# Holding expert 1's weight loads on GpSimd behind the last pair's row copies and two late transposes, in a sparse attention kernel with a routed mixture of experts

## The chip, the cores and the metric

The kernel runs on one core of one Trainium2 chip. The metric is the device time of one execution in microseconds (us), lower is better. Before the change three runs took 671.94, 671.15 and 670.29 us, median 671.15.

The engines are named as the profile names them: PE is TensorE (PEld its weight loads), DVE VectorE, ACT ScalarE, POOL GpSimd, SP SyncE. GpSimd and SyncE issue the DMAs that matter here: GpSimd those that load from DRAM with a cast to 16 bits, SyncE the small copies within the on-chip memory (SBUF) and the transposes by DMA. A name such as L464 is a line of the kernel before; the lines after the changed place stand 11 lower in the changed file.

## What is computed

Attention over 4 batches x 8 heads x 768 positions of width 64, in which each query sees its neighbours at a distance under 16 and one summary for each of 24 blocks of 32 positions (the maximum of the keys, the mean of the values). Then a mixture of 8 experts over all 3072 rows, in which every expert runs on every row and the weights of the routing come from eight rounds of Sinkhorn normalization:

```python
mask_l = np.abs(pos[:, None] - pos[None, :]) < window          # window 16
scores_s = scale * einsum('bhsd,bhnd->bhsn', q, k_sum) + log(block)
a = softmax(concat([where(mask_l, scores_l, -1e9), scores_s]))
x = matmul(a, concat([v, v_sum]))                              # to (3072, 512)
P = exp(x @ w_gate - max)
for _ in range(8):
    P /= P.sum(1, keepdims=True) + 1e-09
    P /= P.sum(0, keepdims=True) + 1e-09
    P *= N / E
for e in range(E):                                             # 8 experts, 512 -> 1024 -> 512
    out += P[:, e:e + 1] * (np.maximum(x @ w1[e], 0) @ w2[e])
```

## The kernel before

**Stages.** The heads are taken in 16 pairs (pair i: two heads of batch i // 4). Pairs 0 to 3 are worked in halves, pairs 4 to 15 whole. Expert 0 needs no routing weight until later, so its two matmuls fill TensorE between the attention's steps (`hps` L221 the hidden layer, `yps` L231 the projection). Up to 128 us or so the profile shows this mixture. Then come the eight Sinkhorn rounds with the end of expert 0 and the beginning of expert 1 woven in, and from 169 us experts 1 to 7, whose products are made with seven half-size products in place of eight (L972 and L978).

**A planner writes the order.** In the first two stages each step is a unit with an engine, an estimated cost, the units it depends on and a priority (`add`). The planner (`Plan.order`) takes the estimates and lists the units in one order; the order of each engine's instructions follows from it and is fixed when the kernel is built. On the chip the engines then wait for each other with semaphores that follow from the tiles that are read and written. `load` adds three units: the issue on POOL, which follows the issue before it, a DMA's duration, and the landing `U[key]`, on which others can depend. Loads are thus issued by GpSimd in the order in which they are added.

**A whole pair** (pairs 4 to 15). Keys and queries are transposed to `kT`, `qT` (from pair 12 on by DMA on SyncE, L354). `scores` makes the neighbour scores (`sg` L383), `score_exp` and `masks` make `em`. `near_values` copies rows of the values from the neighbouring 128-row chunks into `Ve`: four DMAs of 10.2 KB on SyncE, two on L414 and two on L416, for the two heads. `Ve` has two buffers, which alternate. `edges` makes the matching products `Ee` on VectorE (L443, L447). `values` sums it up in `av`: L458 with `em`, then L464 with `Ee` and `Ve`, so that L464 needs all four copies. `normalize` (L546, L547) writes `xs`, which has two buffers for whole pairs: pair i writes where pair i - 2 wrote, once that one has been transposed to `xT`. For pairs 10 to 14 this transpose is a DMA on SyncE (`x_dma`, L358); pair 15's is made on TensorE (`tx` L554) and copied by ScalarE. SyncE's queue has, at the end: `xT` of pair 11, four copies of pair 14, `xT` of pair 12, four copies of pair 15, `xT` of pair 13, `xT` of pair 14.

After the last pair, `logits` (`lp` L568) reads all of the last batch's `xT`; ScalarE makes `P_sb` of it (L572), with which the Sinkhorn rounds begin: row sums and reciprocals on VectorE (L1169, L1170), a product on GpSimd (L1173), column sums on VectorE (L1177), their total on TensorE (`sink` L1182), its reciprocal on VectorE (L1185) and a product on GpSimd (L1190).

**Expert 1's weights.** They are the last loads on GpSimd: `load_w1(1, i)` for i = 0 to 3 (two DMAs of 128 KB each, L197) and `load_w2(1)` (one of 1024 KB, L208). Ahead of them stands `hold`: four one-element copies on GpSimd that read `qT` of pairs 12 to 15 (L885), and so wait until those transposes have landed. On VectorE the sums for the half-size products follow the last normalization: `w1_sum` of the four groups (reading `w`, writing `ws`) and `x_sum` (L919 `xTs`), in this order: groups 0 and 1, the first `x_sum`, group 2 with the second `x_sum` in it, group 3; then the row sums of Sinkhorn. The tiles `xTs`, `ws` and `hf` lie where the attention's tiles lay, `held` among them. TensorE's first products of expert 1 are `pa` (reading `w`) and `pb` (reading `ws` and `xTs`).

Of the kernel before, what the change touches and what calls it, by code (L numbers as in the profile page):

```python
# [10 lines left out]
BF16 = mybir.dt.bfloat16  # L11
# [23 lines left out]
class Plan:  # L35
# [13 lines left out]
    def add(self, eng, cost, fn, deps=(), prio=0.0, opens=(), uses=(), lag=0.0, shape=None):  # L49
        u = Unit(eng, cost, fn, [d for d in deps if d is not None], prio, list(opens), lag, shape)  # L50
        for b in list(opens) + list(uses):
            b.users.append(u)
        if uses and eng != "PE":
            u.prio -= 100.0
        self.waiting.append(u)
        return u
# [80 lines left out]
def kernel(  # L137
# [10 lines left out]
    nc = tc.nc  # L148

    B, H, S, D = q.shape  # L150
# [7 lines left out]
    NP = (B * H) // 2  # L158
    PB = H // 2
# [5 lines left out]
    VD = D + 1  # L165
# [15 lines left out]
    xT = persist.tile([128, KD, N], FP16)  # L181
# [11 lines left out]
    def load_w1(e, i):  # L193
        t = w1s[e, i] = wpool.tile([128, KD, 2, 128], FP16, tag="w1", name="w1", bufs=5)
        for h in range(2):
            f = h * (F // 2) + 128 * i
            nc.gpsimd.dma_start(out=t[:, :, h, :],  # L197
                                in_=moe_w1[e].rearrange("(dk p) f -> p dk f", p=128)[:, :, f:f + 128])
# [7 lines left out]
    def load_w2(e):  # L206
        w2s[e] = wpool.tile([128, KF, DM], FP16, tag="w2", name="w2")
        nc.gpsimd.dma_start(out=w2s[e][:], in_=moe_w2[e].rearrange("(fk p) d -> p fk d", p=128))  # L208
# [28 lines left out]
    NE = 2  # L237
# [8 lines left out]
    attn = early.enter_context(tc.tile_pool(name="attn", bufs=1))  # L246
    aps = early.enter_context(tc.tile_pool(name="aps", bufs=1, space=PSUM))
    if True:

        ident = attn.tile([128, 128], BF16, name="ident")  # L250
        held = attn.tile([1, 1], BF16, name="held")
        band = attn.tile([128, LIVE], BF16, name="band")
        m_blk = attn.tile([128, 4 * (G - 1) + 128], BF16, name="m_blk")
        qT = [attn.tile([128, W + S + W], BF16, name=f"qT{i}") for i in range(NB)]
# [10 lines left out]
        V_e = [attn.tile([128, G, 2 * VD], BF16, name=f"Ve{i}") for i in range(NE)]  # L265

        plan = Plan({"m": 3, "s": NS, "a": NA})
        add = plan.add
# [319 lines left out]
        def keep_busy(n):  # L588

            t = bank("m", "idle")  # L590
            for _ in range(n):
                nc.tensor.matmul(t[:], lhsT=zeros[:], rhs=zeros[:, None, :].to_broadcast([128, 4, 128]), start=True, stop=True)
# [74 lines left out]
        U = {}  # L667
        last = [None, None]

        def load(key, fn, issue, us, deps=(), late=False):  # L670
            last[0] = add("POOL", issue, fn, [last[0], *deps])
            last[1] = add("DMA", us, None, [add("RING", 0, None, [last[0]], lag=0.8), last[1]])
            U[key] = add("LAND", 0, None, [last[1]], lag=1.0 if late else 0.4)
# [209 lines left out]
        def hold():  # L883
            for r in range(12 % NB, NB):
                nc.gpsimd.tensor_copy(out=held[0:1, 0:1], in_=qT[r][0:1, W:W + 1])  # L885

        last[0] = add("POOL", 0.3, hold, [last[0]] + [U["kT", i, 1] for i in range(12, NP)])
        for i in range(4):
            load(("w1n", i), lambda i=i: load_w1(1, i), 0.85, 1.3)
        load("w2n", lambda: load_w2(1), 0.85, 5.0)  # L890
        plan.idle = (0.22, lambda: keep_busy(1), U["rl", 0, 0])
        attention = {u for u in plan.waiting if u.fn is not None} - set(zero)
# [11 lines left out]
    if True:  # L904
# [32 lines left out]
        def weight1(what, e, i):  # L937
            if what in ("S1", "S2", "S4"):
                return ws1[e, i][:, "S1 S2 S4".split().index(what), :, :]
            k = KH if what in ("A12", "A22") else 0  # L940
            return w1s[e, i][:, k:k + KH, int(what in ("A21", "S3", "A22")), :]

        def w1_sum(e, i, n):
            if n == 0:
                ws1[e, i] = fast.tile([128, 3, KH, 128], FP16, tag="ws1", name="ws1", bufs=5)
            m = {w: weight1(w, e, i) for w in "A11 A12 A21 A22 S1 S2 S3 S4".split()}
            f, o, a, b = ((plus, "S1", "A21", "A22"), (sub, "S2", "S1", "A11"), (sub, "S3", "A11", "A21"),
                          (sub, "S4", "A12", "S2"))[n]
            f(m[o], m[a], m[b])
# [209 lines left out]
        def bridge():  # L1159
# [39 lines left out]
            X, Wt = {}, {}  # L1199
# [5 lines left out]
                                  [X.get((j, n - 1))] + hs0, 990.0 + 100 * j + n)  # L1205
            for i in range(4):
                for n in range(4):
                    Wt[i, n] = add("DVE", 0.3, lambda i=i, n=n: w1_sum(1, i, n), [Wt.get((i, n - 1))],
                                   980.0 + 5 * i + n)
            step2 = None  # L1210
            for n in range(4):
# [2 lines left out]
            for i in range(4):  # L1214
                f = made[1, 0, i] = group(1, 0, i)
                a, b, g = Buffer("ab"), Buffer("ab"), Buffer("g")
                k5, k2 = Buffer("c5"), Buffer("c2")
                d = {}

                def op(name, eng, us, deps, opens=(), uses=()):  # L1220
                    d[name] = add(eng, us, f[name], [d[x] if isinstance(x, str) else x for x in deps],
                                  1000.0 + PRI[i], opens=opens, uses=uses)

                op("p1", "PE", 0.44, [], [a])
                op("seed", "ACT", 0.58, ["p1"], [g], [a])
                op("p5", "PE", 0.44, ["p1", Wt[i, 0], X[0, 0]], [b])
                op("c5", "ACT", 0.58, ["p5"], [k5], [b])
                op("p2", "PE", 0.44, ["seed"], (), [a])
                op("r11", "ACT", 0.58, ["p2"], (), [a])
                op("p6", "PE", 0.44, ["seed", Wt[i, 1], X[0, 1]], (), [g])  # L1230
                op("c2", "ACT", 0.58, ["p6"], [k2], [g])
                op("p3", "PE", 0.44, ["c5", Wt[i, 3]], (), [b])
                op("c12", "DVE", 0.68, ["p3", "c2"], (), [b, k2])
                op("p7", "PE", 0.44, ["c2", X[0, 2]], (), [g])
                op("c22", "DVE", 0.68, ["p7", "c5"], (), [g, k5])
                op("p4", "PE", 0.44, ["c22", X[0, 3]], (), [g])
                op("r21", "ACT", 0.58, ["p4"], (), [g])
                op("r12", "DVE", 0.3, ["c12"])
                op("r22", "DVE", 0.3, ["c22"])
                op("s1", "DVE", 0.42, ["r12", "r22"])  # L1240
                op("s3", "DVE", 0.42, ["s1", "r11"])
                op("s2", "DVE", 0.42, ["s1"])
                op("s4", "DVE", 0.42, ["s2", "r21"])

        groups = [(e, j, i) for e, j in steps for i in range(4)]
        LAG = 4
        made, PRI, PW = {}, (5.05, 5.5, 6.05, 6.5), 1007.0
        bridge()
        for u in course:
            if u.fn is not None:  # L1250
# [5 lines left out]
        for n in range(LAG, len(groups)):  # L1256
# [3 lines left out]
            e, j, i = groups[n]  # L1260
# [48 lines left out]
        last = [pair(*groups[len(groups) - LAG + n], spare=bool(n % 2), c1_at=c1s[n], tail=True) for n in range(LAG)]  # L1309
# [49 lines left out]
```

## Time and profile before

| What | us |
|---|---|
| median of three runs | 671.15 |
| the profiled execution, its own time | 674.88 |
| the span in it, first to last instruction | 673.2 |
| TensorE busy in the span | 661.4 |
| VectorE, ScalarE, GpSimd busy | 581.9, 399.7, 129.5 |
| first `w1` issue of expert 1 on GpSimd | 94.54 |
| pair 15's four row copies issued | 102.44 to 104.56 |
| `av` L464 of pair 15 starts | 116.04 |
| first `w1_sum` on VectorE | 117.88 |
| first `pa` of expert 1 on TensorE | 128.10 |

Times inside the span are counted from its start. Timelines have the start, the duration, the engine, the line, what is done (out<-in) and how often; in brackets the idle time ahead and what ended it. The page cuts the span into 40 slices of 16.8 us:

```profile
PE   8999998999999999999999999999999999999996
DVE  8889897677799988998799988998899879998885
POOL 8699440122101010201010010101020101100001
DMA  9999989000513050311422051305031132201224
```

The DMA engines are nearly full for the first six slices, some 100 us, and mostly empty behind. VectorE is busy at 60 to 90% throughout, TensorE nearly all the time.

### The profile page before, as it was taken

The numbers are of one execution on the slowest core, as the hardware profiler recorded it, in microseconds if no ns is written. First come the engines' busy times: TensorE is split into PE (matmuls) and PEld (weight loads), VectorE is DVE, ScalarE is ACT, GpSimd is POOL, SyncE is SP. The second block draws the span as 40 slices with busy tenths as digits, with TensorE's granted clock in tenths as the row PEclk, the third lists the DMA queues.
The fourth block names the chain that finished last, engine by engine and source line by source line (L and its number), as shares of the span: only waits on it lengthen the run. The fifth ranks groups of instructions, "written<-read, shape, count | busy, mean of one in ns | idle before, by whom it ended". The sixth has DMA issues, their size and how long they took to land.

```text
span 673.2 us, 13510 instructions
## 1 busy us (share of the span) xinstructions
PE 661.4 (98%) x5077; PEld 436.4 (65%) x5077; DVE 581.9 (86%) x1475; ACT 399.7 (59%) x782; POOL 129.5 (19%) x175
## 2 busy tenths in 40 slices
PE   8999998999999999999999999999999999999996
PEld 4766655555666666666666666666666666666665
DVE  8889897677799988998799988998899879998885
ACT  6776674565777765555655565555555565556551
POOL 8699440122101010201010010101020101100001
PEclk9999999999999999999999999999999999999999
DMA  9999989000513050311422051305031132201224
GB/s 159 184 150 147 143 97 142 1 1 1 78 11 39 1 79 1 36 14 20 61 23 25 1 79 12 37 1 79 1 36 14 27 52 23 26 1 56 86 80 157
DMA packets 124033, 36.75 MB, mean 55 GB/s; under 512 B 110144, under 2 KB 121152, under 8 KB 123968
## 3 DMA queue, kind: packets, MB, share of 16 engines
q0 software_dynamic: 104128, 25.93, 41.3%
q1 hardware_dynamic: 18880, 9.22, 6.7%
q8 instruction: 40, 0.66, 0.4%
q10 hardware_dynamic: 960, 0.74, 0.3%
q14 instruction: 25, 0.20, 0.1%
HBM read 52.45 MB, written 6.29 MB: 87 GB/s over the span
## 4 chain that ended last, share of the span: by engine, by line
PE 88%; DVE 6%; DMA 5%; issue 0%; ACT 0%; DVEq 0%; ACTq 0%
PE xy L978 37%; PE pg L972 16%; PE pa L972 11%; PE pb L972 11%; PE yps L231 5%; PE hps L221 4%; DMA Ve<-vx 3%; DMA kT<-kst 1%; DVE xs L547 1%; DMA vx<-in_v_dram 1%; PE sg L383 1%; PE tkq L349 1%; PE tx L554 0%; DVE km L377 0%; PE vs L393 0%
## 5 line engine op out<-in xcount | busy, mean ns | idle before, releaser
L978 PEld LDWEIGHTS <-hf 128*128 128x128 f16 x2352 | 230.1, 98 | 95.8 <-issue 0.8
L978 PE MATMUL xy<-w,hf 128*128 128x256 f16 x1312 | 183.4, 273 | 0.0
L978 PE MATMUL xy<-ws,hf 128*128 128x256 f16 x984 | 147.6, 273 | 0.1
L212 ACT ACTIVATE hf<-pg 128x512 f16<-128x512 f32 x84 | 50.1, 597 | 151.3 <-PE pg L972 151.2
L1114 DVE SCALAR_TENSOR_TENSOR out_acc<-xy,P_sb,out_acc 128x512 f32<-128x512 f32 x164 | 115.0, 742 | 2.1 <-PE xy L978 2.1
L919 DVE TENSOR_TENSOR hf<-hf 128x512 f16<-128x512 f16 x252 | 100.2, 425 | 8.9 <-DVE hf L922 0.5
L972 PE MATMUL pa<-xT,w 128*128 128x512 f16 x336 | 99.9, 379 | 0.0
L972 PEld LDWEIGHTS <-w 128*128 128x128 f16 x672 | 65.8, 98 | 43.5
L922 DVE TENSOR_TENSOR hf<-pb,c 128x512 f16<-128x512 f32 x84 | 58.1, 691 | 36.8 <-PE pb L972 34.5
L197 POOL DMA_DIRECT2D w<-in_moe_w_dram x56 | 41.7, 756 | 220.1 <-PE pg L972 191.7
L972 PEld LDWEIGHTS <-ws 128*128 128x128 f16 x504 | 49.3, 98 | 25.1
L1006 ACT COPY c<-pg 128x512 f32<-128x512 f32 x84 | 49.2, 586 | 22.4 <-PE pg L972 22.4
L922 DVE TENSOR_TENSOR hf<-pg,c 128x512 f16<-128x512 f32 x84 | 57.1, 679 | 0.7 <-PE pg L972 0.7
L212 ACT ACTIVATE hf<-pa 128x512 f16<-128x512 f32 x84 | 50.6, 603 | 0.9 <-PE pa L972 0.9
L991 ACT COPY pg<-pa 128x512 f32<-128x512 f32 x84 | 47.9, 570 | 4.9
L972 PE MATMUL pg<-xT,w 128*128 128x512 f16 x168 | 50.0, 379 | 0.0
L972 PE MATMUL pb<-xTs,ws 128*128 128x512 f16 x168 | 50.0, 379 | 0.0
L972 PE MATMUL pg<-xTs,ws 128*128 128x512 f16 x168 | 50.0, 379 | 0.0
L972 PE MATMUL pb<-xT,ws 128*128 128x512 f16 x168 | 50.0, 379 | 0.0
L972 PE MATMUL pg<-xTs,w 128*128 128x512 f16 x168 | 50.0, 379 | 0.0
L999 ACT COPY c<-pb 128x512 f32<-128x512 f32 x84 | 49.8, 593 | 0.0
L221 PE MATMUL hps<-xT,w 128*128 128x384 f16 x256 | 48.9, 326 | 0.0
(150 smaller groups left out, 829.9 us busy)
## 6 DMA issues: line engine op xcount, KB each, us to landing
w<-in_moe_w_dram POOLq DMA_DIRECT2D x8, 1024.0 KB, 9.5
w<-in_moe_w_dram POOLq DMA_DIRECT2D x56, 128.0 KB, 3.4
out_dram<-out_acc SPq DMA_DIRECT2D x20, 256.0 KB, 2.0
vx<-in_v_dram POOLq DMA_DIRECT2D x16, 192.0 KB, 5.8
qst<-in_q_dram POOLq DMA_DIRECT2D x31, 96.0 KB, 5.0
kst<-in_k_dram POOLq DMA_DIRECT2D x24, 96.0 KB, 5.4
w<-in_moe_w_dram POOLq DMA_DIRECT2D x2, 512.0 KB, 9.3
Ve<-vx SPq DMA_DIRECT2D x48, 10.2 KB, 4.6
```

The lines of the kernel that those rows point to most:

```text
L197: nc.gpsimd.dma_start(out=t[:, :, h, :], in_=moe_w1[e].rearrange("(dk p) f -> p dk f", p=128)[:, :, f:f + 128])
L212: nc.scalar.activation(out=out, in_=in_, func=AF.Relu, bias=0.0, scale=1.0)
L221: nc.tensor.matmul(hp[:, 0:n], lhsT=w1s[e][:, dk, 128 * f:128 * (f + 1)], rhs=xT[:, dk, t0:t0 + n], start=(dk == 0), stop=(dk == KD - 1))
L231: nc.tensor.matmul(yp[:], lhsT=h[:, f, c * 128:(c + 1) * 128], rhs=w2s[e][:, f, :], start=(f == 0), stop=(f == KF - 1))
L919: nc.vector.tensor_tensor(out=out, in0=in0, in1=in1, op=ALU.subtract)
L922: nc.vector.tensor_tensor(out=out, in0=in0, in1=in1, op=ALU.add)
L972: nc.tensor.matmul(bank[:], lhsT=w[:, dk, :], rhs=x[:, dk, :], start=start and dk == 0, stop=dk == KH - 1, skip_group_check=True)
L978: nc.tensor.matmul(bank, lhsT=a(f)[:, 128 * c:128 * (c + 1)], rhs=w[:, f, :], start=start and f == 0, stop=f == FH - 1, skip_group_check=True)
L991: nc.scalar.copy(out=B["g"][:], in_=B["a"][:])
L999: nc.scalar.copy(out=B["c5"][:], in_=B["b"][:])
L1006: nc.scalar.copy(out=B["c2"][:], in_=B["g"][:])
L1114: nc.vector.scalar_tensor_tensor(out=acc, in0=src, scalar=P_sb[:, t, e:e + 1], in1=acc, op0=ALU.mult, op1=ALU.add)
```

## The change

`held` grows from one element to 128 partitions x 1. Two new functions read more into it on GpSimd. `hold_near` reads, for each of the two heads, one column of the 32 rows of `Ve` that pair 15's copies write, and then calls `hold_x(12)`, which reads one element of pair 12's `xT`. It stands ahead of the four `w1` loads. `hold_x(14)` reads one element of pair 14's `xT` and stands between the `w1` loads and the `w2` load. Each copy waits for the DMAs that write what it reads, and what stands behind it on GpSimd waits with it. For the planner the new units depend on the landings of those DMAs, and `w1_sum` and `p1` of expert 1 now depend on the landing of their `w1` load.

```diff
-        held = attn.tile([1, 1], BF16, name="held")
+        held = attn.tile([128, 1], BF16, name="held")
...
+        def hold_near():
+            for j in range(2):
+                p = 64 + 32 * j
+                nc.gpsimd.tensor_copy(out=held[p:p + 32, 0:1], in_=V_e[(NP - 1) % NE][p:p + 32, 1, VD * j:VD * j + 1])
+            hold_x(12)
+
+        def hold_x(i):
+            nc.gpsimd.tensor_copy(out=held[0:1, 0:1], in_=xT[0:1, i % PB, i // PB * S:i // PB * S + 1])
+
         last[0] = add("POOL", 0.3, hold, [last[0]] + [U["kT", i, 1] for i in range(12, NP)])
+        last[0] = add("POOL", 0.4, hold_near, [last[0], U["near", NP - 1], U["x", 12]])
         for i in range(4):
             load(("w1n", i), lambda i=i: load_w1(1, i), 0.85, 1.3)
+        last[0] = add("POOL", 0.2, lambda: hold_x(NP - 2), [last[0], U["x", NP - 2]])
         load("w2n", lambda: load_w2(1), 0.85, 5.0)
...
-                    Wt[i, n] = add("DVE", 0.3, lambda i=i, n=n: w1_sum(1, i, n), [Wt.get((i, n - 1))],
+                    Wt[i, n] = add("DVE", 0.3, lambda i=i, n=n: w1_sum(1, i, n), [Wt.get((i, n - 1)), U["w1n", i]],
...
-                op("p1", "PE", 0.44, [], [a])
+                op("p1", "PE", 0.44, [U["w1n", i]], [a])
```

## The prediction

> **What bounds the kernel now.** I read the page first, then the waits of TensorE, the chain of waits, the timeline around the longest wait and the granted clock by microsecond. The page's busy line and its chain line:
>
> ```profile
> PE 661.4 (98%) x5077; PEld 436.4 (65%) x5077; DVE 581.9 (86%) x1475; ACT 399.7 (59%) x782; POOL 129.5 (19%) x175
> PE 88%; DVE 6%; DMA 5%; issue 0%; ACT 0%; DVEq 0%; ACTq 0%
> ```
>
> TensorE is busy for 661.4 of 673.2 us, so a change can gain only where it idles or runs slowly. The waits of TensorE (who waited for whom: total us, times, longest) name one wait that matters:
>
> ```profile
> PE av L464 <- DMA Ve<-vx: 2.9, 1, 2.9
> PE idle L592 <- DVE vx L600: 1.1, 1, 1.1
> PE tx L554 <- DVE xs L547: 0.3, 1, 0.3
> ```
>
> `av` (L464) of pair 15 waits 2.9 us for that pair's row copies into `Ve` (L414 and L416). In the chain of waits (start, us, what) the last pairs' copies are the two longest pieces of this stretch:
>
> ```profile
> 98.11 6.43 DMA Ve<-vx
> ...
> 104.56 11.35 DMA Ve<-vx
> 115.91 0.14 issue
> 116.04 0.40 PE av L464 x3
> ```
>
> Such a copy need not take 11 us. The DMA issues between 85.5 and 88.2 us, while GpSimd's queue was empty, and between 102.2 and 105 us, while it carried expert 1's weights (KB each, median us to landing):
>
> ```profile
> Ve<-vx SPq DMA_DIRECT2D x4, 10.2 KB, 1.9
> ...
> Ve<-vx SPq DMA_DIRECT2D x4, 10.2 KB, 11.8
> ```
>
> The timeline shows when those weights are issued (GpSimd) and what else waits: a normalization on VectorE, 2.34 us for the `xT` transpose of pair 12, which holds the `xs` buffer that pair 14 needs:
>
> ```profile
> 94.08 0.25 POOL L885 COPY held<-qT 1x1 bf16<-1x1 bf16 x1 [6.17 <-DMA qT<-qst]
> 94.54 5.94 POOL L197 DMA_DIRECT2D w<-in_moe_w_dram  x8 [0.21 <-issue]
> 100.40 0.96 POOL L208 DMA_DIRECT2D w<-in_moe_w_dram  x1
> ...
> 112.58 0.56 DVE L547 TENSOR_TENSOR xs<-av,rc 128x384 f16<-128x384 f32 x1 [2.34 <-DMA xT<-xs]
> 113.86 1.21 SPq L358 DMA_TRANSPOSE xT<-xs  x1
> ```
>
> Last the busy time by microsecond: window, its length, PE, PEld, DVE, ACT and POOL busy, then the granted clock.
>
> ```profile
> 115.00:116.00 1.00, 0.00 (x0) 0.00 (x0) 0.00 (x0) 0.00 (x0) 0.00 (x0) 1.00 0.99 193
> 116.00:117.00 1.00, 0.96 (x14) 0.79 (x15) 0.49 (x2) 0.00 (x0) 0.00 (x0) 1.00 0.04 6
> 117.00:118.00 1.00, 1.00 (x5) 0.38 (x3) 0.96 (x4) 0.00 (x0) 0.00 (x0) 0.54 0.00 0
> 118.00:119.00 1.00, 1.00 (x4) 0.34 (x3) 0.96 (x5) 0.59 (x1) 0.00 (x0) 0.50 0.00 0
> 119.00:120.00 1.00, 1.00 (x6) 0.56 (x5) 0.96 (x5) 0.00 (x0) 0.00 (x0) 0.50 0.00 0
> 120.00:121.00 1.00, 1.00 (x8) 0.58 (x6) 1.00 (x3) 0.52 (x1) 0.00 (x0) 0.75 0.00 0
> ```
>
> The wait has a second price: about one microsecond after it TensorE falls to half clock until 120.5 us, and counts as busy meanwhile. Lost are 0.46 + 0.50 + 0.50 + 0.25 = 1.71 us.
>
> **The change, part by part.** The built programs hold the same instructions in the same order on TensorE, VectorE, ScalarE and SyncE; GpSimd alone has four copies more. The new planner dependencies (`w1n`) thus move nothing. Of the waits one changes its meaning: the first `x_sum` on VectorE, which overwrites memory that `held` lies in, waited for the fourth `held` copy and now waits for the eighth.
>
> *Removed: the traffic of expert 1's weights between 96 and 115 us.* Pair 15's copies are issued at 102.44 to 104.4 us as before, since the first waits for TensorE's `av` of pair 13. Quiet copies take 1.9 us; copies queued right behind a transpose took 3.8 (median of those issued between 92.4 and 96.2 us). Pair 12's transpose is issued just ahead, at 100.76, so I take 3.8: landed by 108.2 (bound from below 106.3). TensorE wants them at 113.08 (the last `av` L458 starts at 112.91), so 4.9 us are spare. The next thing it needs there is pair 15's edge products, which stand behind the normalization of pair 14. Pair 12's transpose, quiet, takes 2.7 to 2.8 us and lands near 103.6, so VectorE's 2.34 us go as well and the edges end at 114.70 - 2.34 = 112.4, before 113.08. So the whole 2.93 us go, and with no gap before it I let the half clock go too: 1.71 us. Sum 4.64 us.
>
> At this place a rule speaks against the second term. The Trainium skill ("TensorE: Matmul & The Clock Gate", Part 1) has the clock fall back to half after at least one idle window of about 3.4 us, in windows that run free of the kernel. The gap here is 2.93 us and the clock was 0.50 behind it, so the trace doesn't agree with the length. By the rule alone the sum would be 2.93 us.
>
> *Added: four copies on GpSimd.* The `held` rows last 0.18 to 0.25 us; four are 0.9 us. They hide in GpSimd's idle 24.76 us before the first Sinkhorn product (L1173, 126.12 us).
>
> *Moved: eight `w1` issues.* GpSimd now waits for pair 15's copies and pair 12's transpose, so 106.3 to 108.2, then issues for 5.94 us: until 112.7 to 114.6 with the copies. Behind the waiting copies stand these loads, then the `w2` load, then Sinkhorn's products. Who needs the weights: VectorE's `w1_sum`, first at 117.88 before, now 2.9 us earlier, at 115.0; the fourth group about 119 to 120.5. Landing took 7.1 us in the median with the row copies and transposes beside it, 7.7 at most; 3.4 was the fastest. The first group lands by 109.8 + 7.1 = 116.9 at worst, the last by 114.6 + 7.7 = 122.3 at worst, near 117 if the traffic moves at the quiet pace. VectorE had 2.49 us free before the Sinkhorn row sums (125.28), and TensorE's `sink` product came 1.9 us after the column sums it needs (127.84 to 129.78). Half a microsecond to two is covered by these 4.4; I take 0.
>
> *Moved into the loads' traffic: the transpose of pair 14.* It is issued 2.34 us earlier, at 111.5, now amid the `w1` loads. Quiet it takes 2.7 us (114.2). Pair 11's, issued 2.2 us after the first `w1` load and beside `w1` traffic alone, took 6.7: 118.2. Pair 12's, with `w2` behind too, took 11.7. Of these the 6.7 is the nearest, since `w2` is now held behind this very transpose. TensorE first reads it in the gate's logits (`lp` L568, 124.26), now at 124.26 - 4.64 = 119.6: 1.4 us spare. VectorE's first `x_sum` (119.75, now 116.8 at the earliest) waits for the last `held` copy, 118.4, so 1.6 us; it comes out of the 2.49 above. Price 0; without cover 0 to 3.6, see the rivals.
>
> *Moved: `w2`.* Issued at 118.4 at the latest, with its own 14.5 us landed by 134. Its first reader on VectorE stood at 154.39, now 149.8. Price 0.
>
> Together: 674.88 (span 673.2 and 1.7 around it) - 4.64 = 670.2 for the profiled execution. The median of the runs, 671.15, lies 3.73 below the profiled time; taking the same 4.64 off it gives **666.5 us**.
>
> **The rivals.**
>
> *The half clock is not in the timed runs.* The three runs spread over 1.65 us, about one such loss. For it: the window is 3.4 us long (117.09 to 120.50) and its phase against the gap may differ. Against: the one trace has it. Gain 2.93: 668.2 us.
>
> *The 3.73 us by which the profiled execution is longer lie in this very stall.* For it: copies of 10 KB behind a full queue are what a disturbed execution delays first. Against: a profile also costs outside, and the queue is as full without one. Gain 4.64 - 3.73 = 0.9: 670.2 us.
>
> *The stall moves to pair 14's transpose.* If it takes pair 12's 11.7 us, it lands at 123.2, and the logits wait 3.6 us. With a half clock behind it that is 5.3 against 4.64 won: 671.8; without, 670.1. Against it: `w2`, which made the queue full to 115 us, is held.
>
> *Slower: the same wait, longer.* `w1`'s loads take the queue from the transpose as `w2` did, and it lands only after 14.5 us (`w2`'s own time), at 126.0. The logits wait 6.4 us, the half clock costs 1.7, and on VectorE `x_sum` and what stands behind it up to the row sums (some 3.5 us) end about 129.7 rather than 120.6. The column sums then end at 132.3, and `sink`, due at 129.78 - 4.64 + 8.1 = 133.2, is just covered: 8.1 - 4.64 = 3.5 slower, 674.6 us. It turns into a loss when the transpose lands later than 122.6 with the half clock, 124.3 without, 11 to 13 us after its issue. Against it: the eight loads moved for 12.8 us from first issue to last landing with everything beside them, and would end by 120 here.
>
> *The hold does not hold* can be left out: the two `Ve` reads cover what all four copies write, and the loads stand behind them on one engine.
>
> **How the numbers follow.** A measurement of this kernel can tell 0.3% from no change, 2.0 us, so faster means under 669.1. Full gain 0.52 (666.5), no half clock 0.22 (668.2), small stall in timed runs 0.10 (670.2), stall moved 0.11 (671), slower 0.05 (674.6). Faster 0.52 + 0.22 = 0.74; same 0.10 + 0.11 = 0.21; slower 0.05. The lower end takes the fastest run before, 670.29 - 4.64, and the two small waits at 93.42 and 104.82 us (0.26 and 0.20) as gone too: 665.2. The upper end takes in the small stall and the milder moved one: 670.4. Left out are the worse half of the moved stall and the slower case, about 0.11.
>
> **What would show it.** Right: `av` L464 of pair 15 starts within 0.3 us of the `av` before it; pair 15's copies land 2 to 4 us after their issue; no 0.50 in the granted clock between 113 and 125 us; `w1` issued from about 107; pair 14's transpose landed by 119; Sinkhorn 4.6 us earlier. Wrong: a wait of `lp` L568 for `xT`, of `sink` for the column sums, or `Ve` still landing after 113; the sum is also wrong if the gap goes and the time falls by 3 us only.

## The result: 0.27% faster, less than half of what was forecast

Twelve runs of each kernel: 671.58 us before (670.29 to 674.23), 669.95 us after (669.43 to 670.59). The ratio is 0.9973, 95% interval 0.9964 to 0.9982, so the change saves 1.2 to 2.4 us. The forecast was a saving of 4.64 us and 666.5 us. The measured time lies inside the forecast range of 665.2 to 670.4 us, near its upper end.

The page of the changed kernel, its busy line, the granted clock in 40 slices and the chain by engine:

```profile
PE 659.0 (99%) x5077; PEld 435.7 (65%) x5077; DVE 582.2 (87%) x1475; ACT 399.7 (60%) x782; POOL 131.8 (20%) x179
...
PEclk9999999999999999999999999999999999999999
...
PE 89%; DVE 7%; DMA 1%; ACT 1%; issue 1%; ACTq 0%; DVEq 0%
```

The span is 667.9 us. In the chain the share of DMA fell from 5% to 1%. TensorE's waits (who waited for whom: total us, times, longest) no longer have a line of `av` L464; the list begins (the first two stand in the span's first 5 us, the third at 64 us):

```profile
PE idle L592 <- DVE vx L600: 1.1, 1, 1.1
PE tkq L346 <- ACT kst L217: 0.4, 1, 0.4
PE tx L554 <- DVE xs L547: 0.3, 1, 0.3
```

The timeline of the changed kernel shows the holds on GpSimd and what they let through; in brackets, the idle time ahead and what ended it:

```profile
104.63 0.39 POOL L890 COPY held<-Ve 32x1 bf16<-32x1 bf16 x1 [11.22 <-DMA Ve<-vx]
...
105.94 1.41 POOL L890 COPY held<-Ve 32x1 bf16<-32x1 bf16 x1 [0.92 <-DMA Ve<-vx]
107.41 0.18 POOL L894 CAST held<-xT 1x1 bf16<-1x1 f16 x1
107.54 5.94 POOL L197 DMA_DIRECT2D w<-in_moe_w_dram  x8
...
112.31 0.35 PE L458 MATMUL av<-vx,em 128*128 128x65 bf16 x6
...
112.49 0.34 PE L464 MATMUL av<-Ve,Ee 128*128 128x130 bf16 x3
...
117.69 0.18 POOL L894 CAST held<-xT 1x1 bf16<-1x1 f16 x1 [4.21 <-DMA xT<-xs]
117.91 0.69 DVE L930 TENSOR_TENSOR xTs<-xT 128x1024 f16<-128x1024 f16 x1 [1.70 <-POOL held L894]
118.16 0.90 POOL L208 DMA_DIRECT2D w<-in_moe_w_dram  x1 [0.28 <-issue]
```

GpSimd stands still for 11.22 us, reads pair 15's rows at 104.63 and 105.94, and issues `w1` only from 107.54. In the list of DMA issues between 101.5 and 104.2 us the row copies now take 1.9 us, where they took 11.8:

```profile
Ve<-vx SPq DMA_DIRECT2D x4, 10.2 KB, 1.9
```

So `av` L464 follows the `av` before it without a wait, 112.49 after 112.31. Behind it, by microsecond (window, its length, busy time of PE, PEld, DVE, ACT and POOL, the granted clock), the clock stays at 1.00:

```profile
115.00:116.00 1.00, 1.00 (x10) 0.52 (x8) 0.96 (x6) 0.71 (x1) 0.00 (x0) 1.00 2.26 138
116.00:117.00 1.00, 1.00 (x6) 0.43 (x5) 0.21 (x2) 0.67 (x2) 0.00 (x0) 1.00 2.07 161
117.00:118.00 1.00, 1.00 (x6) 0.49 (x5) 0.09 (x1) 0.12 (x1) 0.18 (x1) 1.00 1.06 114
```

What the prediction named as signs of being right is there: no wait, no half clock, copies that land even sooner than in the 2 to 4 us expected, `w1` issued from 107.54, pair 14's transpose landed by 119, and Sinkhorn's first `sink` product even 5.3 us earlier. Between the two profiles the span fell by 673.2 - 667.9 = 5.3 us, more than was forecast. But the profiled execution of the kernel before, 674.88 us, is longer than all twelve of its runs here, while that of the changed kernel, 669.62 us, is one of its ordinary ones. What the experiments had to settle is how large the stall is in an ordinary execution of the kernel before.

### The profile page after: what moved, and what is told of

Its sections match the earlier page's. It is cut to its first block, busy times and chain, and to the rows that moved or that the text cites. A ratio compares the mean times of both kernels' runs of the same rounds, so it can differ in the third digit from the quotient of the medians.

```text
span 667.9 us, 13518 instructions
## 1 busy us (share of the span) xinstructions
PE 659.0 (99%) x5077; PEld 435.7 (65%) x5077; DVE 582.2 (87%) x1475; ACT 399.7 (60%) x782; POOL 131.8 (20%) x179
## 4 chain that ended last, share of the span: by engine, by line
PE 89%; DVE 7%; DMA 1%; ACT 1%; issue 1%; ACTq 0%; DVEq 0%
PE xy L989 37%; PE pg L983 16%; PE pa L983 11%; PE pb L983 11%; PE yps L231 5%; PE hps L221 5%; DVE xs L547 1%; DMA kT<-kst 1%; PE sg L383 1%; PE tkq L349 1%; DVE em L435 1%; DVE km L377 1%; DVE h L214 0%; DVE kh L375 0%; PE tx L554 0%
```

## The experiments

Two theories stood against each other. In the first, the first profile of the kernel before caught an unusually long stall, and in most executions the stall is short: the change removes all of it, but it is worth less. In the second, the stall of that profile is the usual one, and the changed kernel gives most of the gain back elsewhere (in the added waits, or in the loads that now come late).

**The kernel before, four more times.** No edit.

> The kernel before, unchanged, with the span and the mean granted clock of each timed run. Theory A (the profiled execution was a long one, in most runs pair 15's row copies land earlier): this profile shows a wait of L464 of 0.5 to 2 us and no half clock behind it, the spans scatter by 2 us or more, and the mean clock is 0.998 to 1.000 in most runs, 0.995 to 0.996 only in the longest. Theory B (the stall of 2.9 us and the half clock of 1.7 us are in every run, and the changed kernel gives 3 us back somewhere): a wait near 2.9 us again, a clock of 0.995 to 0.997 in nearly every run. Time as before, 671.6.

> The kernel before, unchanged, one more profile. With before (wait of L464 2.93 us, half clock behind it) and before_again (0.59 us, no half clock) it is a third sample of the wait. Theory A (the wait varies from execution to execution, mostly 0.5 to 2 us): a wait in that range, no half clock, pair 15's copies landed between 113 and 115. Theory B (2.9 us in most): 2.5 us or more.

> The kernel before, unchanged, for one more profile. If a short wait is the usual thing and the long one of the first profile rare: L464 of pair 15 waits 0.5 to 0.8 us, no half clock between 113 and 125 us, profiled execution 671 to 672 us. If the first profile was an ordinary one: a wait of 2.5 us or more with a half clock behind it, 674 to 675 us.

> The same once more, with the same two expectations: 671 to 672 us with a wait of 0.5 to 0.8 us, or 674 to 675 us with a wait of 2.5 us or more and a half clock.

The twelve further runs gave 672.21 us, ratio 1.0008 (0.9989 to 1.0026) to the kernel before on their chip; the four profiled executions took 671.23, 671.14, 671.29 and 672.12 us. In the first of them the timeline shows the same chain of events as in the first profile, only shorter:

```profile
111.99 0.56 DVE L547 TENSOR_TENSOR xs<-av,rc 128x384 f16<-128x384 f32 x1 [1.49 <-DMA xT<-xs]
...
113.27 0.19 DVE L443 TENSOR_TENSOR Ee<-er,band 32x80 bf16<-32x80 bf16 x1
...
113.91 0.20 DVE L447 TENSOR_TENSOR Ee<-er,band 32x80 bf16<-32x80 bf16 x1
...
113.94 0.52 PE L464 MATMUL av<-Ve,Ee 128*128 128x130 bf16 x3 [0.59 <-DVE Ee L443]
```

Here the row copies are not what comes last. The normalization of pair 14 waits 1.49 us for the transpose of pair 12, the edges behind it are finished late, and `av` waits 0.59 us for them. The last copy landed at about 113.8, only 0.1 us ahead of the edges, so both were late. Waits of the fourth, in which the row copies came last again:

```profile
PE av L464 <- DMA Ve<-vx: 0.9, 1, 0.9
PE tx L554 <- DVE xs L547: 0.7, 2, 0.4
```

All seven profiles of the two kernels, from the timeline: the wait of L464, whether the clock halves behind it, and the time from the last group of `vs` (L393, some 10 us ahead of the stall) to the first `sink` (behind it), then from there to the end of the span. The rows of `vs` and `sink` are, for the execution of 671.23 us and for the changed kernel of 669.62 us:

```profile
102.91 0.52 PE L393 MATMUL vs<-vx,m_blk 128*128 128x128 bf16 x6
...
125.96 0.28 PE L1182 MATMUL sink<-csum_sb,col_en 128*128 128x8 f32 x2
```

```profile
102.20 0.52 PE L393 MATMUL vs<-vx,m_blk 128*128 128x128 bf16 x6
...
124.34 0.28 PE L1193 MATMUL sink<-csum_sb,col_en 128*128 128x8 f32 x2
```

| Kernel, execution | wait of L464 | half clock behind it | `vs` to `sink` | `sink` to the end |
|---|---|---|---|---|
| before, first profile | 2.93 | 3.41 us | 26.96 | 543.6 |
| before, 671.23 us | 0.59 | no | 23.05 | 543.5 |
| before, 671.14 us | 0.73 | no | 23.20 | 543.5 |
| before, 671.29 us | 1.23 | no | 23.69 | 543.6 |
| before, 672.12 us | 0.87 | no | 24.12 | 543.6 |
| after, 669.62 us | none | no | 22.14 | 543.6 |
| after, 669.64 us | none | no | 22.13 | 543.6 |

The last column does not change: nothing behind the stall gained or lost by the change, within 0.1 us. The stretch with the stall shrinks by 4.8 us against the first profile, but by 0.9, 1.1, 1.6 and 2.0 us against the other four, 1.4 in the mean. (In the first three of these four some 0.33 us more than the wait is lost; the products of L464 no longer start while those of L458 run, and the first three take 0.52 us in place of 0.34. In the last of the four `tx` starts late as well, since `xs` of pair 15 waited 1.35 us for the transpose of pair 13.) In the profiles of the five versions below in which TensorE doesn't wait here, this stretch takes 22.12 to 22.14 us too. What else the spans differ by lies ahead of `vs`, which starts at 102.15 to 102.91 us in these seven (102.66 in the first profile, 102.20 in that of the changed kernel); no wait that the change removes lies there. The first theory held. Why the stall is so long in some executions stays open.

**The changed kernel again.** No edit.

> The changed kernel, unchanged, in more runs. If the change takes out both a short wait in every execution and a long wait with a half clock in the few slow ones: a median 1.2 to 2.0 us under that of the kernel before on this chip, every run under 672.5 us and none with a mean clock of 0.997 or less. If the slow executions have another cause, some of these runs reach 674 us or more too.

669.73 us (669.41 to 671.01, 12 runs), 671.93 before; ratio 0.9969 (0.9954 to 0.9983). The difference of the medians, 2.2 us, is just above the expected 2.0; the rest came as expected. The kernel before has 89 runs with a granted clock on record. In 14 of these the mean granted clock was 0.997 or lower, and these 14 took 673.78 to 676.52 us. The other 75 took at most 673.47 us, median 671.53. Of the 24 runs of the changed kernel none is in the first group, and the longest took 671.01 us. So the change is worth some 671.53 - 669.95 = 1.6 us in an ordinary execution, and it also takes away the long ones, one in six. These long runs weren't profiled; that each of them has the long stall with the half clock of the first profile is likely from their clock, but not shown. The kernel with more load below has the same sign: its profiled execution, mean clock 0.996, has such a half clock.

**Which of the two holds matters.** First the changed kernel without the second hold:

```diff
-        last[0] = add("POOL", 0.2, lambda: hold_x(NP - 2), [last[0], U["x", NP - 2]])
```

> The changed kernel without its last hold: the w2 load follows the four w1 loads at once. By the prediction's steps pair 14's transpose (6.5 us in the changed kernel, landed at 117.6) then has w2 behind w1 in its way, as pair 12's had before (11.7 us): landed at 118 to 123, against its first reader on TensorE at 119.0. If it lands after 119: a wait of L568 of up to 4 us, time 670 to 673. If the hold of w2 is worth nothing: same time as the changed kernel, 670.0, no wait on TensorE.

670.39 us (670.12 to 671.57, 10 runs), ratio 0.9968 (0.9952 to 0.9983), no wait of TensorE in this stretch. Pair 14's transpose took 6.6 us with `w2` right behind `w1`, and 6.5 with `w2` held. The second hold does nothing here that could be measured. Then the reverse, `w1` as early as in the kernel before, and only `w2` behind both holds:

```diff
-        last[0] = add("POOL", 0.4, hold_near, [last[0], U["near", NP - 1], U["x", 12]])
         for i in range(4):
             load(("w1n", i), lambda i=i: load_w1(1, i), 0.85, 1.3)
+        last[0] = add("POOL", 0.4, hold_near, [last[0], U["near", NP - 1], U["x", 12]])
         last[0] = add("POOL", 0.2, lambda: hold_x(NP - 2), [last[0], U["x", NP - 2]])
```

> Expert 1's w1 loads as early as in the kernel before; only w2 waits for pair 15's copies and for the transposes of pairs 12 and 14. If w1's traffic is what delays pair 15's copies: they land later than 113 again, wait of L464 1 to 3 us, time about 671.5 as before. If it was w2 behind w1: the copies land by 109 to 111, no wait, time about 670.0 as in the changed kernel. I hold the second likelier, 6 to 4, since w1's last landing stood at 107.4 and w2's at 115 in the profile before.

670.42 us (669.89 to 671.08, 7 runs), ratio 0.9967 (0.9954 to 0.9981), again no wait. Its DMA issues between 101.5 and 104.8 us (KB each, median us to landing):

```profile
Ve<-vx SPq DMA_DIRECT2D x4, 10.2 KB, 5.3
xT<-xs SPq DMA_TRANSPOSE x1, 6.6
```

With `w1` in front and no `w2`, the copies take 4.6 to 5.9 us and land by 109.2, some 3.9 us before `av` L464 reads them (113.15). So it was the one 1 MB load of `w2`, issued at 100 us, that made the stall, and `w1` could have stayed where it was.

**The added wait on VectorE.** The changed kernel, with the copies that read `xT` writing to a tile of their own, which `x_sum` doesn't overwrite, so that the 1.70 us wait should go:

```diff
+    held_x = const.tile([1, 1], BF16)
...
-            nc.gpsimd.tensor_copy(out=held[0:1, 0:1], in_=xT[0:1, i % PB, i // PB * S:i // PB * S + 1])
+            nc.gpsimd.tensor_copy(out=held_x[0:1, 0:1], in_=xT[0:1, i % PB, i // PB * S:i // PB * S + 1])
```

> The changed kernel with the copies that read pair 12's and pair 14's xT written to a tile that no later tile overlaps, so that the first x_sum on VectorE no longer waits for the last hold. Prediction's step: that wait (1.7 us in the changed kernel's profile) is covered by VectorE's slack before the row sums, so the wait of L930 for held goes and the time stays at 670.0 within 0.5 us. Rival: the wait sets the Sinkhorn rounds, then 1 to 1.7 us faster.

670.93 us (670.05 to 672.17, 10 runs), ratio 0.9978 (0.9966 to 0.9990): nothing is gained. The wait is gone from the profile, and the stretch from `vs` to `sink` takes 22.13 us, as before the edit: the wait was covered, as its price of 0 said. The expected 670.0 within 0.5 us was missed all the same, and the median lies half a microsecond above that of the two versions on the same chip. In the profiled execution `vs` starts only at 104.26 us; 1.19 us of that delay is a gap at another place, `yps` L232 at 76.8 us, that no other profile shows. Whether the other runs have it isn't known.

**The size of `w2`'s pieces.** The kernel before, without any hold, but with expert 1's `w2` in four DMAs of 128 columns each, which are pieces of 256 B in place of 1 KB:

```diff
-        nc.gpsimd.dma_start(out=w2s[e][:], in_=moe_w2[e].rearrange("(fk p) d -> p fk d", p=128))
+        for d in range(0, DM, DM // 4 if e == 1 else DM):
+            n = slice(d, d + (DM // 4 if e == 1 else DM))
+            nc.gpsimd.dma_start(out=w2s[e][:, :, n], in_=moe_w2[e].rearrange("(fk p) d -> p fk d", p=128)[:, :, n])
```

> The kernel before, but w2 of expert 1 comes in four DMAs of 128 columns each: the same bytes in pieces of 256 bytes rather than 1024. Theory of turns (in the traces before, while w2 moves at 150 pieces a microsecond, the transpose moves at 150 too, piece against piece): with pieces of 256 bytes pair 12's transpose ends about 2 us earlier and pair 15's copies land by 111 to 112: no wait of L464, time 670.0 to 670.5. Theory of bytes (the queue shares bandwidth, whatever the pieces): copies land at 113 to 116 as before, wait 0.5 to 3 us, time 671.5 to 672.2. A third way: small pieces delay the row copies themselves as w1's did (5 to 6 us each), wait 1 us or more.

669.84 us (669.41 to 670.19, 10 runs), ratio 0.9971 (0.9953 to 0.9988): the whole gain of the change without a hold. Pair 12's transpose took 8.7 us in place of 11.6 and landed at 108.3, the copies 6.4 to 7.1. The edit changes two things at once: the pieces are smaller, and the load is issued as four DMAs from 99.70 to 103.96 us, in place of one at 100 us. No run separates them. The packets of the two queues (packets, MB, share of the engines' time) speak for the size. In the kernel before (execution of 671.23 us), 106 to 109 us, while `w2` and pair 12's transpose move together, and below it 112 to 113 us, when `w2` is over:

```profile
q0 software_dynamic: 460, 0.47, 92.0%
q1 hardware_dynamic: 457, 0.12, 29.5%
```

```profile
q1 hardware_dynamic: 674, 0.16, 122.2%
q0 software_dynamic: 8, 0.01, 3.7%
```

GpSimd's queue (q0) and SyncE's (q1) moved packets one for one, 460 and 457, although one moves 1 KB a packet and the other a quarter of it. SyncE's queue moved 152 packets per us, and 674 in one us once `w2` had ended. With `w2` in small pieces, 110 to 112 us, while it moves together with pair 13's transpose:

```profile
q0 software_dynamic: 579, 0.15, 82.1%
q1 hardware_dynamic: 578, 0.15, 71.9%
```

Close to one for one again, but 289 per us each, nearly twice as many. From 104 to 106 us, while pair 12's transpose moves, it is 505 to 601. Not all stretches are so: in the same execution, 106 to 109 us, GpSimd's queue moved 1658 packets against 360. SyncE's packets there are smaller (0.05 MB in 360), as those of the row copies are, and the row copies of the changed kernel, with no load beside them, move no more than 288 in 2 us (103 to 105 us). Whether that sets the share there stays open.

**More of the same load.** The kernel before with one more load of 1 MB behind `w2` (half of expert 2's, into memory that isn't in use yet):

```diff
+        last[0] = add("POOL", 0.85, lambda: nc.gpsimd.dma_start(
+            out=out_acc[:, NT - 4:NT, :], in_=moe_w2[2].rearrange("(fk p) d -> p fk d", p=128)[:, 0:4, :]), [last[0]])
```

> The kernel before with one load more right behind w2 on GpSimd: 1 MB of expert 2's w2, uncast, into the last four tiles of out_acc, which expert 0 overwrites later. It doubles the traffic that the row copies meet. If that traffic sets the wait: pair 15's copies land 2 to 5 us later than in the kernel before (116 to 119), wait of L464 3 to 6 us, a half clock of 3.4 us behind it in nearly every run (mean clock 0.995 to 0.997), time 675 to 678. If the copies are held by something else: time 671.5 to 672.2 and a wait of 0.5 to 3 us.

676.13 us (672.70 to 678.49, 10 runs), ratio 1.0057 (1.0032 to 1.0082). It is slower, but by another wait than was expected. The copies landed by 112.6 and L464 didn't wait. The transpose of pair 13, which stands behind them on SyncE, took 13.3 us, to 118.4, and held the `xs` buffer of pair 15:

```profile
118.47 0.56 DVE L547 TENSOR_TENSOR xs<-av,rc 128x384 f16<-128x384 f32 x1 [4.95 <-DMA xT<-xs]
...
119.09 0.50 PE L554 MATMUL tx<-ident,xs 128*128 128x128 f16 x3 [3.71 <-DVE xs L547]
```

Behind this wait of 3.71 us the granted clock (sixth number behind the window's length) is at half again, for 3.41 us, as in the first profile:

```profile
119.00:120.00 1.00, 0.72 (x6) 0.46 (x7) 0.93 (x5) 0.00 (x0) 0.00 (x0) 0.51 0.00 0
120.00:121.00 1.00, 1.00 (x6) 0.45 (x5) 0.96 (x5) 0.68 (x1) 0.00 (x0) 0.50 0.00 0
121.00:122.00 1.00, 1.00 (x4) 0.38 (x3) 1.00 (x4) 0.12 (x1) 0.00 (x0) 0.50 0.00 0
122.00:123.00 1.00, 1.00 (x5) 0.37 (x4) 1.00 (x4) 0.59 (x1) 0.00 (x0) 0.78 0.00 0
```

The queues again moved packets one for one: while the added load, which isn't cast, moves beside that transpose (113 to 115 us), it is 168 packets (0.65 MB) to 167 (0.04 MB). Which of the three transfers on SyncE (the transposes of pairs 12 and 13, the copies of pair 15) comes too late thus differs from one execution to the next; that one of them does is due to the 1 MB loads. The clock of the runs agrees: eight of these ten have a mean of 0.993 to 0.997.

**Both remedies together.** The edit of "`w1` as early as in the kernel before" and that of the four pieces:

> Expert 1's w1 early as before, its w2 behind the second hold only, and in four pieces. No wait of TensorE is left in this stretch in any of the variants so far, so if their common gain is all that the order of these loads can give: ratio 0.996 to 0.998, as for each part alone. If something that the profiles do not show as a wait (turns on the queues late in the loads) still costs: under 0.995.

669.75 us (669.22 to 670.55, 12 runs), ratio 0.9969 (0.9956 to 0.9983): as each alone. With no wait left in this stretch there is nothing more to win in the order of these loads, and no version beats the changed kernel by a measurable margin. None of the 49 runs of the five versions without a wait here (all but that with more load) has a mean clock of 0.997 or lower.

## Why the prediction was wrong in size

**The removed wait, the step that failed.** The prediction had the mechanism: the stall of L464 is the work of expert 1's loads, and it goes when they are held. What failed is the sum's first number. "So the whole 2.93 us go, and with no gap before it I let the half clock go too: 1.71 us" is true of that profiled execution (its stretch fell by 4.8 us), and the next step, "taking the same 4.64 off" the median, carried it over to runs of another kind. In four other executions the whole loss was 0.9 to 2.0 us, without a half clock. The median's gain was 1.6 us. What came last there also differed: in three of the four it was pair 14's normalization and the edges behind it, with the copies landing 0.1 to 0.4 us ahead of them; the prediction had counted that second path as going too, so the change removed both. That the measured time lies in the range at all is owed to its upper end, which was set to take in the small stall, a rival with a chance of 0.10.

**The sign that was passed over.** The profiled execution was 3.73 us longer than the median and longer than each of the three runs. The prediction set this against the median by subtraction, and gave the rival in which those 3.73 us lie in this very stall a chance of only 0.10, with "a profile also costs outside" against it. Six further profiled executions of the two kernels contradict this: they took 671.14 to 672.12 us before and 669.62 and 669.64 after, among the ordinary runs of their kernels. That rival named the cause, and its 0.9 us is the smallest of the four measured losses.

**The half clock.** The Trainium skill ("TensorE: Matmul & The Clock Gate", Part 1) has the clock fall back after at least one idle window of about 3.4 us. The traces have it behind gaps of 2.93 and 3.71 us, for 3.41 us each time, and not behind gaps of 0.59 to 1.23 us. The length of the low clock agrees with the Trainium skill's window; the gap that brings it can be shorter than the Trainium skill has it. Where between 1.23 and 2.93 us it begins wasn't tried, nor whether a gap of one length always brings it.

**What was costed at nothing.** The held `w1` (issued from 107.54, "about 107" in the prediction) cost nothing: from `sink` to the end nothing moved, and with `w1` early the stretch ahead of `sink` takes the same 22.14 us. Pair 14's transpose took 6.5 us, where pair 11's 6.7 was taken, and landed at 117.6, 1.4 us ahead of `lp`. The wait of `x_sum` was 1.70 us for a predicted 1.6, and was covered. The row copies took 1.9 us in place of 3.8, though pair 12's transpose (2.8 us) stood right ahead of them; the price was too high, on the safe side.

**What the prediction got wrong without a price.** It took 6.7 us for pair 14's transpose "since `w2` is now held behind this very transpose". Without that hold it took 6.6, so the reason was not needed. The two small waits at 93.42 and 104.82 us (`vs` L393, 0.26 us, and `ss` L470, 0.20 us), which the lower end of the range took as gone too, are still there at 92.96 and 104.37 us, with 0.27 and 0.20.

## What to carry over

Compare the profiled execution's own time with the timed runs first: where it is longer than all of them, the stall that it shows may be the very thing that makes it longer, and a saving is then worth its share in an ordinary execution, not its size in the trace. Each of the four further profiles of the unchanged kernel would have shown it. And a small transfer that must be in time can be rescued not only by delaying the large load on the other queue, but also by cutting that load into several DMAs of smaller packets.

## What the runs showed of the hardware

- While a load and a transpose moved together, their two queues moved packets one for one in several stretches (460 to 457, 579 to 578, 168 to 167), whatever their size: a queue of 1 KB packets then took four times the bytes of one with 256 B packets. Pair 12's transpose took 11.6 us there, and 2.8 us without the loads. Beside row copies the counts were uneven (1658 to 360).
- In the one kernel the cost of the same stall varied fivefold between executions, from 0.9 to 4.8 us: the wait was 0.59 to 2.93 us, and behind the longest one the clock halved for 3.41 us, which cost 1.71 us more. Of the runs with a clock on record, the executions with a mean clock up to 0.997 (14 of 89) were the only ones over 673.5 us.
